# Layer norm, token mixer and MLP on one core: one tile's transpose goes from TensorE to the DMA queue, and every engine gets an explicit order list

## The chip, the cores and the metric

The kernel runs on one core of a Trainium2 chip. The metric is the device time in microseconds (us), the median of three runs. A profile of one execution gives the span from the first to the last instruction, and all rows quoted here are from it.

## What is computed

x is 2048 tokens by 512 features, in bf16; w1 and w2 are 512 by 512, w3 is 512 by 1792, w4 is 1792 by 512.

```
h  = gelu(layernorm(x) @ w1)
g0, g1, g2, g3 = the four quarters of h's features, shifted along the tokens by 1, -1, 2, -2 (zeros come in)
x1 = x + concat(g0, g1, g2, g3) @ w2
out = x1 + gelu(layernorm(x1) @ w3) @ w4
```

## The kernel before

The tokens are cut into 16 tiles of 128. For every tile t there is a first layer norm, numbered t, and a second, numbered 16 + t. A layer norm is a chain of small steps: the statistics (on DVE as bn_stats, L432, and bn_aggr, L434; or for the numbers in STAT_ACT as passes of ACT, L411 and L416, finished on DVE at L421, L424 and L428), the reciprocal root rstd on POOL (L439), then the norm itself: on DVE (L461), or, after a small step nmr (L466), on ACT (L470) or POOL (L473). NORM says which engine, NMR where nmr runs.

A normed tile must be transposed before it can be an operand. Two ways exist. `pe_transpose` turns it on TensorE by four 128x128 transposes (L506) into PSUM, from which EVAC's engine copies it (L514, "both" is half each on ACT and DVE). Or `ln` issues a DMA transpose on SP's queue (L479), named tp and the number. Tiles named in SCRIPT with sa/sb, ty or tp are turned on TensorE: 0 to 7 in this kernel. The other 24 go by DMA.

TensorE's work has five kinds. `mm_up` makes a layer's product with w1 or w3 (L642) for a group of tiles (GROUPS: in the first layer tiles 0 to 4 alone, 5 and 6 together, 7 alone, 8-9, 10-11, 12-15; in the second 0-1, 2-3, 4-7, 8-11, 12-15), in blocks of up to 1024 columns of PSUM, and ACT takes each block through gelu (L657). up1_6 is the first layer's product of group 6, that is of tile 7; up1_7, up1_8 and up1_9 are those of tiles 8-9, 10-11 and 12-15. Tile 0 is done another way round (L544, L610). `mm_mix` multiplies the shifted h of tile t with w2 (L697), and DVE adds x (L709 or L713, named x1_t), after which tile t's second layer norm can run. Because of the shifts, mix t reads the h of its neighbours too. `mm_down` multiplies with w4 (L731), DVE adds x1 (L739), SP sends the result out (L742). Tile 15's down product is cut into pieces of 256, 160 and 96 columns (TAIL). Nine products with zeros stand first on TensorE (warm, L756).

PSUM has three pairs of banks for products and gelu (y_ps) and two banks for mixes, downs and single transposes (o_ps); they are used in turn, so a later step waits for the reader of an earlier one.

SCRIPT sets the order of TensorE's work. LOADS sets the order of the loads on SP (x at L384, weights at L393), with numbers like x4-5 for one load of two tiles. Everything else was ordered by a planner: `order` gives each operation a due time counted back from TensorE's list, BIAS shifts some of them, and `place` then runs through a modelled time (durations, queue and landing models) and picks for each engine the ready operation that is due first. The result is one list per engine; each engine runs its list strictly in order, and waits stand in front of the instruction that needs them (`emit`).

Of the kernel before, what the change touches and what calls it, by code (L numbers as in the profile page):

```python
# [6 lines left out]
P = 128  # L7
# [7 lines left out]
class Op:  # L15


    def __init__(self, name, eng, fn, reads, writes, dur, queue):
        self.name, self.eng, self.fn = name, eng, fn
        self.reads, self.writes = list(reads), list(writes)  # L20
        self.dur, self.queue = dur, queue
        self.idx = 0
        self.descs = 8.0
        self.prio = 1e9
        self.first = None

class Program:

    HOP = {"pe": 200.0, "dve": 155.0, "act": 220.0, "pool": 120.0, "sp": 70.0}
    LOOK = {"dve": 300.0, "act": 300.0}
    DUE = 179877.0
    BEGIN = {"sp": 30.0, "act": 150.0, "pe": 400.0, "dve": 150.0, "pool": 450.0}
    ENTRY = 1900.0
    COLD, RESTART = 4300.0, 800.0
    RING = 150.0
    LAG = {"load": 750, "tp": 350}

    def __init__(self):  # L40
        self.ops = []
        self.lines = []

    def add(self, eng, name, fn, reads=(), writes=(), dur=100.0, queue=None):
        op = Op(name, eng, fn, reads, writes, dur, queue)
        op.idx = len(self.ops)
        self.ops.append(op)
        return op

    def line(self, names):  # L50

        self.lines.append(list(names))

    def order(self):
# [25 lines left out]
        order_only = set()  # L80
        for names in self.lines:
            for a, b in zip(names, names[1:]):
                assert named[a].eng == named[b].eng, (a, b)
                order_only.add((named[a].idx, named[b].idx))
        last = None
        pe_pos = 0
        for op in self.ops:
            if op.eng == "pe":
                if last is not None:
                    preds[op.idx].add(last.idx)  # L90
                last = op
                op.prio = pe_pos
                pe_pos += 1
        order_only = {(a, b) for a, b in order_only if a not in preds[b]}
        for a, b in order_only:
            preds[b].add(a)
        succs = [set() for _ in self.ops]
        for i, d in enumerate(preds):
            for j in d:
                succs[j].add(i)  # L100
        left = [len(s) for s in succs]
        stack = [i for i, n in enumerate(left) if n == 0]
        seen = 0
        while stack:
            i = stack.pop()
            seen += 1
            for j in preds[i]:
                if self.ops[j].eng != "pe":
                    self.ops[j].prio = min(self.ops[j].prio, self.ops[i].prio)
                left[j] -= 1  # L110
                if left[j] == 0:
                    stack.append(j)
        assert seen == len(self.ops), "cycle"
        if self.DUE:

            topo, left = [], [len(d) for d in preds]
            stack = [i for i, n in enumerate(left) if n == 0]
            while stack:
                i = stack.pop()
                topo.append(i)  # L120
                for j in succs[i]:
                    left[j] -= 1
                    if left[j] == 0:
                        stack.append(j)
            due, t = {}, self.DUE
            for op in self.ops:
                if op.eng == "pe" and not op.name.startswith("warm"):
                    due[op.idx] = t
                    t += op.dur
            for i in reversed(topo):  # L130
                op = self.ops[i]
                late = due.get(i, 1e9)
                for j in succs[i]:
                    o = self.ops[j]
                    hop = 70.0 if op.queue else (self.HOP[op.eng] if o.eng != op.eng else 120.0)
                    work = (2300.0 if op.queue == "tp" else op.dur + 1850.0) if op.queue else op.dur
                    late = min(late, o.prio - hop - work)
                op.prio = late
        for op in self.ops:
            op.prio += BIAS.get(op.name, 0.0)  # L140
            if op.first is not None:
                op.prio = op.first
        for names in self.lines:
            for a, b in reversed(list(zip(names, names[1:]))):
                named[a].prio = min(named[a].prio, named[b].prio - 1e-3)

        self.preds = preds
        out = self.place(succs, order_only)
        for a, b in order_only:
            preds[b].discard(a)  # L150
        return out

    def place(self, succs, order_only):

        npend = [len(d) for d in self.preds]
        ready = [0.0] * len(self.ops)
        cands = {e: [] for e in ENGINES}
        for op in self.ops:
            if npend[op.idx] == 0:
                cands[op.eng].append(op)  # L160
        free = dict(self.BEGIN)
        rings = {"sp": [], "act": []}
        fed = {}
        clock = moved = last = turned = self.total = 0.0
        out = []

        def finish(limit):
            nonlocal clock
            while True:
                heads = {e: r[0] for e, r in rings.items() if r}  # L170
                if not heads:
                    return None
                live = [e for e in heads if heads[e][0] <= clock]
                later = min([h[0] for h in heads.values() if h[0] > clock], default=1e18)
                if not live:
                    if later > limit:
                        return None
                    clock = later
                    continue
                first = min(live, key=lambda e: heads[e][1])  # L180
                step = heads[first][1] * len(live)
                ends = clock + step <= min(later, limit)
                if not ends:
                    step = min(later, limit) - clock
                for e in live:
                    heads[e][1] -= step / len(live)
                clock += step
                if ends:
                    return rings[first].pop(0)[2]
                if clock >= limit:  # L190
                    return None

        def release(op, o, at):
            npend[o.idx] -= 1
            if at is not None:
                ready[o.idx] = max(ready[o.idx], at)
            if npend[o.idx] == 0:
                cands[o.eng].append(o)

        def land(op):  # L200
            nonlocal moved, last, turned
            if op.queue == "tp":
                turned = max(clock + 500.0, op.start + 2450.0, last + 500.0, turned + 480.0)
                at = turned + self.LAG["tp"]
            elif op.name.startswith("out"):
                at = clock + 300.0
                self.total = max(self.total, at)
            else:
                moved += op.dur
                at = clock + 600.0 + min(600.0, 0.3 * moved) + (600.0 if op.dur > 1400.0 else 0.0)  # L210
                at += 50.0 if moved <= 1200.0 else self.LAG["load"] - 300.0 if moved <= 4000.0 else self.LAG["load"] if moved <= 11000.0 else self.LAG["load"] + 650.0
            if op.queue != "tp":
                last = max(last, at)
            op.landed = at
            for j in succs[op.idx]:
                if (op.idx, j) not in order_only:
                    release(op, self.ops[j], at + 30.0)

        while len(out) < len(self.ops):
            while True:  # L220
                best = None
                for e in ENGINES:
                    if cands[e]:
                        t = max(free[e], min(ready[o.idx] for o in cands[e]))
                        if best is None or t < best[0]:
                            best = (t, e)
                op = finish(best[0] if best else 1e17)
                if op is None:
                    break
                land(op)  # L230
            t, e = best
            look = self.LOOK.get(e, 1.0)
            op = min((o for o in cands[e] if ready[o.idx] <= t + look), key=lambda o: (o.prio, o.idx))
            cands[e].remove(op)
# [674 lines left out]
```

## Time and profile before

| what | us |
|---|---|
| median of three runs | 135.59 |
| the runs | 135.73, 135.45, 135.59 |
| span of the profiled execution | 133.7 |
| granted TensorE clock, mean | 1.000 |

The profile page gives, per engine, the busy time, its share of the span and the instructions; then the chain of work that ended last, followed back from the end, with shares by engine and by line; then groups of instructions by line. The view of waits lists for one engine the line that waited, the line that released it, the total, the count and the longest. The timeline lists instructions in order of time: start, time to the end of the last of a merged row, engine, line, operation, tiles, count. TensorE's rows overlap, since a product's end is modelled and the next starts before it: there the distance from start to start is what a step takes. Of the DMAs there is a list of issues (out<-in, queue, operation, count, size, median us from issue to landing) and of queues (packets, MB, share of all 16 DMA engines' time in the stretch asked for). Since names of tiles do not tell which tile of 128 tokens a row is, single operations are found by their order on their engine.

| DMAs on SP before, in order | issued at |
|---|---|
| x 0-1, x 2, w1 in two halves | 0.08 to 1.56 |
| x 3, x 4-5, w2 in two halves, x 6, x 7, x 8-10, w3 | 2.16 to 5.54 |
| x 12-13, x 11 | 6.07, 6.68 |
| two transposes, x 14-15 | 14.67, 15.99, 17.29 |
| 16 transposes | 17.91 to 40.79 |
| w4 in two halves | 42.13, 42.75 |
| the other transposes, and outputs | from 43.36 |

### The profile page before, as it was taken

Reading aid. Unit: us, or ns where it says so; the run is one execution under the profiler, and the core shown is the slowest. Engines: PE = TensorE matmul, PEld = TensorE weight load, DVE = VectorE, ACT = ScalarE, POOL = GpSimd, SP = SyncE. Lnnn points to the kernel's source line nnn. Section 1 sums busy time; section 2 is a strip of 40 time slices with the busy share of each in tenths; the row PEclk is TensorE's granted clock in tenths of the full one; section 3 lists DMA queues with packets and bytes.
Section 4 is the critical chain, followed back from the end, with each engine's and each line's share of the span. In section 5 each row is a group of like instructions: output and inputs, shape, how many; then the busy total and the mean of one; then the engine's idle time right before and its main releaser. Section 6 shows DMA issues by size and latency. Waiting matters only on the chain.

```text
span 133.7 us, 2004 instructions
## 1 busy us (share of the span) xinstructions
PE 130.6 (98%) x776; PEld 71.8 (54%) x789; DVE 50.9 (38%) x138; ACT 56.0 (42%) x89; POOL 30.9 (23%) x69
## 2 busy tenths in 40 slices
PE   8999999999999999999999999999999999999994
PEld 3488768874488444444444444444444444444464
DVE  1899998887550830052260003322220000232223
ACT  5699998858657155520025553000006663000000
POOL 2447567696544120012022003100000000000000
PEclk9999999999999999999999999999999999999999
DMA  4999966745442991002211000311111000111112
GB/s 134 329 349 401 237 150 95 83 89 107 98 99 49 295 329 40 0 0 43 77 42 39 0 0 0 78 39 44 39 42 37 0 0 0 39 44 39 39 39 78
DMA packets 21305, 12.19 MB, mean 91 GB/s; under 512 B 13872, under 2 KB 20784, under 8 KB 21296
## 3 DMA queue, kind: packets, MB, share of 16 engines
q1 hardware_dynamic: 20864, 11.93, 32.7%
q10 hardware_dynamic: 432, 0.13, 0.4%
q8 instruction: 6, 0.10, 0.3%
q14 instruction: 3, 0.02, 0.1%
HBM read 6.82 MB, written 2.10 MB: 67 GB/s over the span
## 4 chain that ended last, share of the span: by engine, by line
PE 94%; DMA 2%; DVE 2%; issue 1%; SPq 0%
PE y_ps L642 46%; PE o_ps L731 36%; PE o_ps L697 10%; DMA x_sb<-in_x_dram 2%; PE y_ps L506 1%; DVE st L432 1%; PE y_ps L544 1%; DVE xn_buf L448 0%; DVE xn_buf L461 0%; DVE o_sb L739 0%; PE o_ps L610 0%; DVE mv L434 0%; SPq L894 0%
## 5 line engine op out<-in xcount | busy, mean ns | idle before, releaser
L642 PE MATMUL y_ps<-xnT,w_sb 128*128 128x512 bf16 (+2 forms) x421 | 63.6, 308 | 0.2
L642 PEld LDWEIGHTS y_ps<-xnT,w_sb 128*128 128x128 bf16 x424 | 38.4, 98 | 24.6 <-DVE mv L434 0.2
L731 PE MATMUL o_ps<-w_sb,h2T 128*128 128x512 bf16 (+3 forms) x248 | 48.7, 355 | 0.2
L657 ACT ACTIVATE h2T<-y_ps 128x1024 bf16<-128x1024 f32 (+1 forms) x29 | 28.6, 993 | 47.2 <-PE y_ps L642 47.1
L731 PEld LDWEIGHTS o_ps<-w_sb,h2T 128*128 128x128 bf16 x252 | 23.6, 98 | 25.2
L739 DVE TENSOR_TENSOR o_sb<-o_ps,x_sb 128x512 bf16<-128x512 f32 (+3 forms) x18 | 11.4, 632 | 45.7 <-PE o_ps L731 45.7
L439 POOL TENSOR_TENSOR rstd<-mv,neghalf 128x1 f32<-128x1 f32 x20 | 11.1, 553 | 35.1 <-DVE mv L434 30.1
L697 PE MATMUL o_ps<-w_sb,hT 128*128 128x512 bf16 x58 | 14.8, 379 | 0.3
L432 DVE BATCH_NORM_STATS2 st<-x_sb 128x6 f32<-128x512 bf16 x20 | 13.5, 676 | 2.6 <-DMA x_sb<-in_x_dram 2.5
L713 DVE TENSOR_TENSOR x_sb<-o_ps,x_sb 128x512 bf16<-128x512 f32 x10 | 6.8, 677 | 14.8 <-PE o_ps L697 14.8
L439 POOL TENSOR_TENSOR rstd<-vpe,neghalf 128x1 f32<-128x1 f32 x12 | 6.7, 558 | 15.6 <-DVE vpe L428 15.5
L473 POOL TENSOR_SCALAR xn_buf<-x_sb,rstd,nmr 128x512 bf16<-128x512 bf16 x12 | 9.2, 764 | 1.0 <-DVE nmr L466 0.4
L657 ACT ACTIVATE hT<-y_ps 128x512 bf16<-128x512 f32 (+1 forms) x10 | 8.1, 806 | 3.1 <-PE y_ps L642 2.9
L697 PEld LDWEIGHTS o_ps<-w_sb,hT 128*128 128x128 bf16 x64 | 6.1, 98 | 5.7
L709 DVE SCALAR_TENSOR_TENSOR x_sb<-o_ps,x_sb 128x512 bf16<-128x512 f32 x6 | 4.1, 681 | 12.1 <-PE o_ps L697 12.1
L416 ACT ACTIVATE junk<-x_sb 128x512 bf16<-128x512 bf16 x12 | 7.5, 622 | 2.1 <-DVE x_sb L709 2.0
L461 DVE TENSOR_SCALAR xn_buf<-x_sb,mv,rstd 128x512 bf16<-128x512 bf16 x13 | 6.1, 471 | 2.7 <-POOL rstd L439 2.0
L470 ACT ACTIVATE xn_buf<-x_sb,nmr,rstd 128x512 bf16<-128x512 bf16 x6 | 4.9, 813 | 0.5 <-POOL nmr L466 0.4
L756 PE MATMUL o_ps<-zeros 128*128 128x512 bf16 x9 | 4.0, 631 | 0.4 <-DVE zeros L363 0.4
L411 ACT ACTIVATE junk<-x_sb 128x512 bf16<-128x512 bf16 x6 | 3.7, 624 | 1.2 <-DMA x_sb<-in_x_dram 1.2
L434 DVE BATCH_NORM_AGGREGATE mv<-st 128x2 f32<-128x9 f32 x20 | 3.8, 192 | 0.3
L506 PE MATMUL y_ps<-ident,xn_buf 128*128 128x128 bf16 x32 | 3.4, 236 | 0.2 <-DVE xn_buf L461 0.2
(34 smaller groups left out, 28.7 us busy)
## 6 DMA issues: line engine op xcount, KB each, us to landing
out_dram<-o_sb SPq DMA_DIRECT2D x15, 128.0 KB, 1.7
w_sb<-in_w_dram SPq DMA_DIRECT2D x1, 1792.0 KB, 10.9
w_sb<-in_w_dram SPq DMA_DIRECT2D x2, 896.0 KB, 6.2
x_sb<-in_x_dram SPq DMA_DIRECT2D x4, 256.0 KB, 3.6
w_sb<-in_w_dram SPq DMA_DIRECT2D x4, 256.0 KB, 4.3
x_sb<-in_x_dram SPq DMA_DIRECT2D x5, 128.0 KB, 4.5
x_sb<-in_x_dram SPq DMA_DIRECT2D x1, 384.0 KB, 5.7
xnT<-xn_buf SPq DMA_TRANSPOSE x24, 2.5
```

Of the source, the lines that this page charges most:

```text
L416: (lambda d: (lambda e: e.activation(d, src, ACT_F.Square, accum_out=sums[:, q, 1:2])))(junk[:, b, :]),
L432: pg.add("dve", f"bnst{q}", lambda e: e.bn_stats(st9[:, q, 0:6], src), reads=rs, writes=[(("st", q), 0)], dur=605)
L439: lambda e: e.tensor_tensor(col(rstd), var, neghalf[:], ALU.pow),
L461: lambda e: e.tensor_scalar(dst, src, mv[:, q, 0:1], rstd[:, q : q + 1], ALU.subtract, ALU.mult),
L470: f = lambda e: e.activation(dst, src, ACT_F.Identity, bias=nmr[:, q : q + 1], scale=rstd[:, q : q + 1])
L473: f = lambda e: e.tensor_scalar(dst, src, rstd[:, q : q + 1], nmr[:, q : q + 1], ALU.mult, ALU.add)
L642: ins = e.matmul(y_ps[:, p, W * i : W * (i + 1)], wsb[:, dc, P * fc : P * (fc + 1)], src[:, dc, P * t0 : P * t0 + W], start=(dc == 0), sto ...
L657: (lambda d, s: (lambda e: e.activation(d, s, ACT_F.Gelu_apprx_tanh)))(dst, ysrc),
L697: ins = e.matmul(dst, hT[:, j, c0 : c0 + P], w2_sb[:, j, :], start=(j == order[0]), stop=(j == order[-1]))
L713: f = lambda e: e.tensor_tensor(x1_sb[:, t, :], dst, x_sb[:, t, :], ALU.add)
L731: ins = e.matmul(dst, h2T[:, fc, P * t : P * (t + 1)], w4_sb[:, fc, cs], start=(fc == 0), stop=(fc == FC - 1))
L739: (lambda d, c: (lambda e: e.tensor_tensor(o_sb[:, oi, c], d, x1_sb[:, t, c], ALU.add)))(dst, cs),
```

## The change

Tile 7 is no longer in SCRIPT as a tile for TensorE, so `ln` issues a DMA transpose for it, tp7. It is the first transpose on SP, behind w3 and two loads of x. The last loads of x (tiles 15 and 13) stand behind five transposes. In SCRIPT tile 7's product comes behind mixes 2, 3, 5 and 4 instead of behind mix 3; tile 6 is turned ahead of the fourth product, tile 5 into a bank of o_ps; the blocks of the second layer's products are named one by one (up2:0.4 is group 0, block from 4 on) and stand between mixes and other products. The planner is gone: `order` keeps the dependencies and checks, and takes the order of SP, ACT, DVE and POOL from written lists (ORDER). AHEAD names the operations that are issued ahead of the entry barrier, the same ones as before. The tables NORM, EVAC, STAT_ACT and NMR move statistics and norms between engines. Below is the core; the lists of ACT, DVE and POOL are cut after the first layer's part, and SP's list is whole.

```diff
-        order_only = set()
-        for names in self.lines:
...
-        out = self.place(succs, order_only)
+        lists = {e: [named[n] for n in ORDER[e].split()] for e in ENGINES if e != "pe"}
+        lists["pe"] = [op for op in self.ops if op.eng == "pe"]
...
+            heads = [lists[e][at[e]] for e in ENGINES if at[e] < len(lists[e])]
+            heads = [op for op in heads if preds[op.idx] <= done]
+            op = min(heads, key=lambda op: (op.name not in AHEAD, ENGINES.index(op.eng)))
...
+NORM = {5: "pool", 7: "act", 8: "act", 9: "pool", 10: "act", 12: "pool", 13: "pool", 14: "pool", 19: "pool", 21: "act", 24: "act", 25: "pool", 26: "act", 27: "pool", 28: "act", 30: "pool", 31: "act"}
+EVAC = {0: "dve", 1: "act", 2: "dve", 3: "both", 4: "both", 5: "dve", 6: "both"}
+STAT_ACT = (0, 5, 7, 9, 10, 12, 16, 18, 20, 22, 24, 25, 26, 27, 28)
+NMR = {5: "pool", 7: "pool", 8: "pool", 9: "pool", 12: "pool", 14: "pool", 19: "pool", 21: "pool", 25: "pool", 26: "pool", 27: "pool", 30: "pool", 31: "pool"}
...
-x0-1 x2 tp2 w1a w1b x3 x4-5 w2b w2a tp5 x6 tp6 x7 x8-10 tp4 w3 x12-13 tp0 x11 tp17 x14-15 tp26 tp5 w4a tp3
-w4b
+x0-1 x2 w1a w1b w2b w2a w3 w4a w4b x4-5 x14 x13 x7 x15 x3 x6 x8-10 x11-12
...
-warm:9 sa:0 sb:0 ty:1 ra:0 rb:0 ty:2 up1:1 th:0 up1:2 mix:0 ty:3 mix:1 ty:4 up1:3 ty:5 up1:4 ty:6 mix:2
-up1:5 ty:7 mix:3 up1:6 mix:5 mix:4 up2:0 up1:7 mix:6 up1:8 mix:7-8 up1:9 mix:10 mix:9 up2:1 mix:13 mix:11
-up2:2 mix:14 down:2 down:1 down:0 mix:12 up2:3 mix:15 down:3 down:5 down:7 down:4 down:6 down:10 up2:4
-down:8 down:11 down:9 down:12-15
+warm:9 sa:0 sb:0 ty:1 ra:0 rb:0 ty:2 up1:1.0 th:0 up1:2.0 ty:3 mix:0 mix:1 ty:4 ty:6 up1:3.0 tp:5 up1:4.0
+up1:5.0 mix:2 mix:3 mix:5 mix:4 up1:6.0 up2:0.0 mix:6 up1:7.0 up2:0.4 up2:0.8 mix:8 up1:8.0 mix:7 up2:0.12
+mix:9 mix:10 up1:9.0 up1:9.2 up2:1.0 up2:1.4 mix:15 mix:13 up2:1.8 mix:12 up2:2.0 mix:11 up2:2.2 mix:14
+up2:1.12 down:0 down:1 down:2 up2:2.4 up2:2.6 up2:2.8 up2:2.10 up2:3.0 up2:2.12 up2:3.2 up2:4.0 up2:3.4 down:7
+down:3 up2:3.6 up2:3.8 up2:4.2 up2:3.10 down:4 up2:4.4 down:5 up2:3.12 up2:4.6 up2:4.8 down:8 up2:4.10 down:11
+down:6 down:10 up2:4.12 down:9 down:12 down:13 down:14 down:15
...
+    "sp": """
+dma_x0 dma_x2 dma_w1a dma_w1b dma_x3 dma_x4 dma_x6 dma_w2b dma_w2a dma_x7 dma_x8 dma_w3 dma_x11 dma_x14 tp7
+tp16 tp17 tp9 tp8 dma_x15 dma_x13 tp11 tp10 tp12 tp15 tp14 tp13 tp18 tp19 tp22 tp23 tp21 tp20 dma_w4b tp26
+dma_w4a tp25 out_dma1_0 tp30 tp28 tp24 tp27 tp31 tp29 out_dma0_0 out_dma3_0 out_dma5_0 out_dma4_0 out_dma7_0
+out_dma2_0 out_dma6_0 out_dma10_0 out_dma8_0 out_dma11_0 out_dma9_0 out_dma13_0 out_dma14_0 out_dma12_0
...
+    "act": """
+warm_gelu sum0 ssq0 ev1 gelur0 ssq5 gelu1_1_0 sum5 gelu1_2_0 ev3act ssq7 sum7 sum9 ev4act ssq16 ev6act
+gelu1_3_0 norm7 ssq9 gelu1_4_0 gelu1_5_0 sum10 ssq18 sum12 norm8 ssq12 gelu1_6_0 ssq20 ssq10 gelu2_0_0 norm10
+ssq22 norm21 gelu1_7_0 gelu2_0_8 gelu2_0_4 ssq24 gelu1_8_0 gelu2_0_12 norm24 ssq26 ssq25 gelu1_9_0 gelu1_9_2
...
+    "dve": """
+zeros bnst1 bnag1 bnst2 norm0_0 norm0_1 norm1 bnag2 ev0_0 msq0 ev0_1 vpe0 norm2 bnst3 bnag3 ev2 bnst4 norm3
+evh0 bnag4 bnst6 msq5 bnag6 vpe5 ev3dve norm4 norm6 x1_0 msq7 ev4dve vpe7 mean16 bnst8 ev6dve ev5 x1_1 msq16
+vpe16 bnst17 bnag17 msq9 norm16 bnag8 vpe9 norm17 x1_2 x1_3 bnst19 bnag19 mean18 x1_5 x1_4 mean20 msq18 bnst21
+msq10 bnag21 bnst11 msq20 vpe20 bnag11 vpe18 msq12 vpe10 bnst14 norm20 x1_6 nmr10 norm11 vpe12 bnst15 mean22
+msq22 bnag15 norm18 vpe22 bnag14 bnst13 norm15 bnag13 x1_8 nmr13 mean24 msq24 norm22 vpe24 nmr24 x1_7 bnst23
...
+    "pool": """
+trip0 trip1 neghalf ident0 epsc pad0 ident1 pad1 rstd1 rstd2 rstd0 rstd3 rstd4 rstd6 rstd5 nmr5 norm5 rstd7
+nmr7 rstd16 rstd17 rstd9 rstd8 nmr9 nmr8 norm9 rstd19 nmr19 norm19 rstd21 rstd20 rstd10 rstd11 rstd18 nmr21
+rstd12 nmr12 norm12 rstd14 rstd15 nmr14 norm14 rstd13 rstd22 norm13 rstd24 rstd23 rstd25 nmr25 norm25 rstd26
...
```

In these lists bnst and bnag are bn_stats and bn_aggr, sum, ssq, mean, msq and vpe the steps of the statistics on ACT and DVE, ev a copy out of PSUM, and dma_x11 the load that begins with tile 11.

## The prediction

> **What bounds it.** I read the busy shares and the chain that ended last first, then what PE waited for, then PE's timeline.
>
> ```profile
> PE 130.6 (98%) x776; PEld 71.8 (54%) x789; DVE 50.9 (38%) x138; ACT 56.0 (42%) x89; POOL 30.9 (23%) x69
> ...
> PE 94%; DMA 2%; DVE 2%; issue 1%; SPq 0%
> ```
>
> ```profile
> PE o_ps L756 <- DVE zeros L363: 0.4, 1, 0.4
> PE y_ps L506 <- DVE xn_buf L461: 0.2, 1, 0.2
> ```
>
> The first fence says that PE is busy for 98% of the span and is 94% of the chain. The second is PE's whole list of waits: 0.4 us before its first instruction and 0.2 us before tile 1 is turned. From 5.12 us to its last product PE waits for nothing. So only work taken from PE, or a shorter head or tail, can make this kernel faster; everything else can only add waits. The timeline of PE gives the price of each step (first column the start, second the time to the modelled end, so the start of the next line is what counts).
>
> ```profile
> 9.64 1.03 PE L697 MATMUL o_ps<-w_sb,hT 128*128 128x512 bf16 x4
> 10.50 0.39 PE L506 MATMUL y_ps<-ident,xn_buf 128*128 128x128 bf16 x4
> 10.72 1.06 PE L642 MATMUL y_ps<-xnT,w_sb 128*128 128x128 bf16 x16
> 11.62 0.39 PE L506 MATMUL y_ps<-ident,xn_buf 128*128 128x128 bf16 x4
> ...
> 13.82 1.91 PE L642 MATMUL y_ps<-xnT,w_sb 128*128 128x256 bf16 x16
> 15.57 0.39 PE L506 MATMUL y_ps<-ident,xn_buf 128*128 128x128 bf16 x4
> ```
>
> From start to start: a mix 0.86, turning a tile 0.22, a first-layer product of one tile 0.89, sixteen products 256 wide 1.75 (eight: 0.87).
>
> **What is removed: 0.22 us.** Tile 7 is no longer turned on PE: four transposes, 0.22 us (10.50 to 10.72), all of it on the path. Its copy out of PSUM (ACT or DVE, under 0.7 us) was beside PE and is worth nothing. The Trainium skill ("TensorE: Matmul & The Clock Gate", Part 4: PE-mode transpose) gives about 275 ns for one 128x128 transpose inside a kernel; by that the change would save 1.1 us. The row shows four in 0.22 us, because each starts 0.056 us after the one before, and the row decides.
>
> The head keeps its end. On DVE bn_stats of tile 2 now runs ahead of the two halves of tile 0's norm, but the same instructions stand before tile 1's norm, so PE's wait still ends at 5.12. Tile 0's copies move from ACT to DVE and end near 5.37 and 5.75; their products started at 5.45 and 5.89, so this costs nothing between bounds of 0 and 0.1. The last four down products and the three pieces of the tail are as before, so the tail is worth 0. The planner is gone from the program text only; no instruction on the chip goes with it.
>
> **What is moved: deadlines.** Up to the second group's product (end 8.55) PE does the same as now. I add the prices above in the new order, without waits: tile 5 is turned at 11.84, up1_5 starts 12.96, mix 2 at 14.70, up1_6 (tile 7) at 18.15, up2_0 (its first block) at 19.05, up1_7 (tiles 8, 9) at 21.66, up1_8 (tiles 10, 11) at 27.75, up1_9 (tiles 12 to 15) at 32.96. Each of these starts now waits for something with little room, and I work out each from rows.
>
> Tile 5's norm moves to POOL, behind the rstd of tiles 6 and 5:
>
> ```profile
> 9.39 0.55 POOL L439 TENSOR_TENSOR rstd<-vpe,neghalf 128x1 f32<-128x1 f32 x1
> 10.04 0.26 POOL L466 TENSOR_SCALAR nmr<-mv,rstd 128x1 f32<-128x1 f32 x1
> ...
> 11.00 0.26 POOL L466 TENSOR_SCALAR nmr<-mv,rstd 128x1 f32<-128x1 f32 x1
> 11.37 0.76 POOL L473 TENSOR_SCALAR xn_buf<-x_sb,rstd,nmr 128x512 bf16<-128x512 bf16 x1
> ```
>
> An rstd is followed by its nmr after 0.65, that by the norm after 0.37, and the norm takes 0.76. Tile 6's bn_aggr ends on DVE near 9.56, so the two rstd start at 9.62 and 10.14, nmr 10.79, norm 11.16 to 11.92, plus 0.07 to PE: **0.15 late**.
>
> Transposes on SP come next. An issue takes 1.31 from one to the next; in an empty queue it lands 2.5 after its issue. Behind copies it is held:
>
> ```profile
> 14.67 1.27 SPq L479 DMA_TRANSPOSE xnT<-xn_buf  x1
> ...
> 22.36 1.27 SPq L479 DMA_TRANSPOSE xnT<-xn_buf  x1
> ...
> 26.01 1.26 SPq L479 DMA_TRANSPOSE xnT<-xn_buf  x1
> ```
>
> ```profile
> x_sb<-in_x_dram SPq DMA_DIRECT2D x1, 128.0 KB, 10.8
> ...
> xnT<-xn_buf SPq DMA_TRANSPOSE x1, 3.4
> ...
> q8 instruction: 1, 0.02, 7.1%
> xnT<-xn_buf SPq DMA_TRANSPOSE x1, 4.2
> ...
> xnT<-xn_buf SPq DMA_TRANSPOSE x1, 2.5
> ```
>
> The second of these fences shows issue to landing (last number). The last x load was issued at 6.7 and landed at 17.5; the transpose of 14.67 landed at 18.07, 0.6 behind it. The one of 26.01 took the plain 2.5, the one of 22.36 took 4.2, in a stretch with an instruction fetch on one DMA engine (7.1% of 16 engines over 1.3 us: that engine's whole time).
>
> In the new list the same bytes stand ahead of the transposes (the three first weights and 14 tiles of x), so the copies again end at 17.5. Tile 7's norm is on ACT, behind 0.48 (gelu), 0.30 (half copy) and 0.61 (statistics pass) steps from 8.87 on; I add them to a norm from 13.17 to 13.98. Then tp7 is issued at 14.03, tp16 15.34, tp17 16.65, tp9 17.96, tp8 19.27. They land at 18.1, 18.5, 19.15, 20.5, 21.8. With 0.06 to PE: tp7 on time for 18.15, tp17 0.15 late for 19.05, tp8 **0.16 late** for 21.66. x15 and x13 are issued behind tp8 and no longer hold it; that is the cover which this order buys. The bound for tp7: if it issued at once it is still held to 18.1; if ACT is 0.5 later it still is; beyond that all five shift alike.
>
> tp11 waits for tile 11's norm on DVE. From the start of tile 3's add (16.79, after mix 3) to the end of that norm stand four adds of 0.65, four bn_stats (2.48 with one wait), three bn_aggr 0.31, a norm 0.32, nine small ones 1.06, nmr 0.13 and the norm's 0.41: 7.31, so 24.1. The small ones are 0.07 each back to back and 0.25 where one reads the one before; these bounds make 0.63 to 2.25 of the nine, and the end 23.7 to 25.3. I take 24.1, nearest to back to back, as most of them read older results. tp11 then issues at 24.13, tp10 25.44, landing 27.93: **0.24 late** for 27.75 (bounds: 0.2 early to 1.4 late). tp12, tp15, tp14, tp13 follow at 1.31 each, the last at 30.68, landing 33.17: **0.27 late** for 32.96. Queued behind are tp18 to tp20, with 0.9 us or more of room.
>
> These are not added: a wait of PE at one place moves PE to where the next only asks for the rest, since the SP queue and DVE run on by their own chains. The largest counts: 0.27 us of waits in all.
>
> Further on I find room. w4's halves are issued near 40.0 and 41.9 and took 5.2 and 7.2 from issue to landing, so 49.1 against the first down at 50.8. The first output, which waits for down 1, stands ahead of six transposes, issued from 58.3 on; tp27, the fourth, lands 64.7 against 66.7. Blocks of up2 on PE take 1.73 and their gelu 1.02, as now. The outputs reuse four buffers in an order that leaves 0.5 us or more. One DMA more (one transpose, and one load more from the new cut of x) is in queues already counted.
>
> **Sum.** -0.22 + 0.27 = +0.05 on the profiled span of 133.73 us. The profile gives no other time for this execution; I take the 1.86 between this span and the median of the runs, 135.59, as unchanged, which makes **135.64**. Anything within 0.27 us (0.2%) is no change for a measurement of this kernel: the three runs spread over 0.28.
>
> **Rivals.** First, the waits are covered: if DVE's small ones run at 0.07 and POOL at the pitch of two rstd, 0.52, only the 0.22 remains, 135.37, still within 0.2%. For it: four of five lateness figures are under 0.25, about my rows' rounding along a chain. Against it: five places would all have to turn out early. It is also the floor, as PE has nothing else to lose, so a clear gain needs the measurement's own spread.
>
> Second, on the other side: an instruction fetch on one DMA engine holds a transpose that PE now waits for. The row of 22.36 prices it: 4.2 - 2.5 = 1.7; the one of 19.15 (3.9, partly behind a load) 1.4 at most. In the stretch from 20 to 22 us there are two fetches of 8 KB now, half the size. tp8 and tp9 move their packets there in the new order, and PE has no room, where today up1_7 starts at 25.5, some 2.5 us after its tiles landed. I take 0.9, between nothing and 1.7: 0.16 + 0.9 - 0.22 = +0.85, 136.4; with the full 1.7 on tp10, 0.24 + 1.7 - 0.22, 137.3. It decides from 0.5 us of lateness on. Against it: a fetch follows the count of instructions, which the new order shifts by some tenths of a us. The Trainium skill ("Runtime: NRT & Kernel Launch", Instruction fetch mechanics) calls crossing a 16 KiB block of instructions mostly hidden, which would price this rival at nothing; the transpose of 22.36 shows otherwise for whoever shares the DMA engine.
>
> Third, the change might not do what it says: tp7 late enough to cost the 0.22 it saves. It is held to 18.1 in any case and up1_6 comes at 18.15 to 18.3, so this needs 0.3 us more on the loads, as when w3 is later: 135.7, inside the forecast's own range.
>
> **Chances.** Forecast 0.45 (135.45 to 135.9), no waits 0.20, a held transpose 0.30, others 0.05. Faster by over 0.2% takes 0.08 from the second and 0.02 from others: 0.10. Slower takes 0.30, 0.05 from the forecast's top and 0.03 from others: 0.38. Same: 0.52. The range leaves out the upper half of the held case and the spread below the floor: 135.3 to 136.8.
>
> **What would show it.** PE with four transposes fewer at L506; a wait of about 0.15 there on POOL near 11.9; waits at L642 on DMAs near 18 to 19, 21.7, 27.8 and 33, summing to 0.3 or less. One wait of 0.7 or more at 21.7 or 27.8, with a transpose that took over 3 us to land, is the second rival. Waits of PE after 40 us, on w4 or on h2T, would be something I have missed.

## The result, and the profile after

The changed kernel takes **136.72 us** (four runs, 136.66 to 136.82) against 135.52 (135.34 to 135.73): a ratio of 1.0092 with an interval of 1.0076 to 1.0108, so it is slower by 1.2 us. That is inside the predicted range (135.3 to 136.8), but at its upper end, on the side of the second rival and not of the forecast, which was no change.

The page of the changed kernel, engine by engine and then the chain by engine:

```profile
PE 131.2 (97%) x772; PEld 71.1 (53%) x785; DVE 48.2 (36%) x145; ACT 58.2 (43%) x96; POOL 28.5 (21%) x66
...
PE 86%; DMA 7%; DVE 2%; SPq 1%; issue 1%
```

What TensorE waited for (line, releaser, total us, times, longest us):

```profile
PE y_ps L477 <- DMA xnT<-xn_buf: 0.8, 2, 0.4
PE o_ps L590 <- DVE zeros L203: 0.4, 1, 0.4
PE y_ps L344 <- DVE xn_buf L287: 0.4, 1, 0.4
```

The chain gives PE 86% where it gave 94%, and DMA 7% where it gave 2%. The new line in the list of waits is the first: two waits of products (L477) for DMA transposes. The timeline of PE says which (start, time to the modelled end, idle time before in brackets):

```profile
18.96 1.06 PE L477 MATMUL y_ps<-xnT,w_sb 128*128 128x128 bf16 x16
20.42 1.91 PE L477 MATMUL y_ps<-xnT,w_sb 128*128 128x256 bf16 x16 [0.40 <-DMA xnT<-xn_buf]
22.17 1.03 PE L531 MATMUL o_ps<-w_sb,hT 128*128 128x512 bf16 x3
23.55 0.72 PE L477 MATMUL y_ps<-xnT,w_sb 128*128 128x256 bf16 x5 [0.35 <-DMA xnT<-xn_buf]
```

These are up1_6 (tile 7, on time), up2_0 and up1_7. The brackets are shorter than what is lost, because a product's modelled end runs past the next one's start: by start-to-start distance up2_0 comes 0.57 late (20.42 instead of 18.96 + 0.89) and up1_7 0.52 (23.55 instead of 22.17 + 0.86). From 24 us to the last product PE does not wait any more.

The whole account of the two profiled executions, by PE's steps: the last product starts 1.67 later. The removed transposes are worth -0.22. Mix 0 waits 0.26 for its half of w2 (landed at 9.75, 8.43 before), tile 5's turn and mix 5 about 0.15 together, up2_0 0.57, up1_7 0.52, and tile 0's products start 0.25 later (5.70 against 5.45). That is 1.53; the rest is small gaps. Not all of it is owed to the change, since the executions of one kernel differ and before's profiled one was a fast one. In every run since, the time is about 1.33 above the span, so its span of 133.73 stands for some 135.1 and not for the median. Its loads came early: w1's first half landed at 4.74, but at 5.08 to 5.67 in 12 of the 13 other profiles told of here, whatever the head of the kernel. And mix 0 waits over 0.1 for w2 in none of the others. The waits for transposes are most of what is left.

SP's queue shows where the two waits begin. Five transposes, tp7, tp16, tp17, tp9, tp8, merged in one row, and the first two of them alone:

```profile
14.46 7.15 SPq L317 DMA_TRANSPOSE xnT<-xn_buf  x5
```

```profile
14.46 3.23 SPq L317 DMA_TRANSPOSE xnT<-xn_buf  x2
```

At the 1.31 per issue of the profile before, five would take 6.5 and two 2.6. The second issue, tp16's, is held: 1.92 instead of 1.27. All that follows is 0.65 later, so tp17 lands at 20.29 while PE stands ready at 19.86; 0.65 earlier it would have been in time. The DMA queues from 14.4 to 18 us (queue, packets, MB, share of 16 engines; then issues, with the median us to landing):

```profile
q14 instruction: 1, 0.01, 1.8%
q8 instruction: 1, 0.02, 1.8%
...
xnT<-xn_buf SPq DMA_TRANSPOSE x3, 3.8
```

Two fetches of instructions, each 1.8% of 16 engines over 3.6 us, so about 1 us of one engine; the 16 KB one starts at 15.59, right ahead of the held issue. Then tp8, issued at 20.35, takes 3.1 to land instead of 2.5. The queues from 21.5 to 23.6 us:

```profile
q14 instruction: 1, 0.01, 0.9%
...
xnT<-xn_buf SPq DMA_TRANSPOSE x1, 3.1
```

The fetch of 8 KB starts at 21.93, in the middle of tp8's packets. Of the 544 packets of transposes that start between 21.5 and 22.85, the median takes 0.02 us; 13 take over 0.3 us, and all of these end at 22.8. Beside the 16 KB fetch it is alike: 14 of tp7's packets take 0.9 to 1.2 us and all end at 17.5, and tp16's issue ends at 17.69.

Is it chance that a held issue has a fetch beside it? In the 14 profiles of the kernels told of here 235 transposes are issued between 12 and 40 us. 27 of the issues took over 1.45 us, and **in each of the 27 a fetch was under way**, in 24 of them one of 16 KB:

| issues of transposes | held (over 1.45 us) | not held |
|---|---|---|
| a fetch of 16 KB under way | 24 | 10 |
| a fetch of 8 KB alone | 3 | 29 |
| no fetch | 0 | 169 |

Of the ten with 16 KB that were not held, seven met the fetch only in their last 0.3 us, two only in their first 0.5, and one took 1.45. The kernel before has one too, 2.27 us at 23.69 beside the fetch of 23.43; no product was due there. Its earlier 16 KB fetch, from 14.10 to 15.16, fell on the first 0.5 us of its first issue and held nothing.

### The profile page after: what moved, and what is told of

Same layout as the page of the kernel before. It is cut to its first block, busy times and chain, and to the rows that moved or that the text cites. A ratio compares the mean times of both kernels' runs of the same rounds, so it can differ in the third digit from the quotient of the medians.

```text
span 135.4 us, 2006 instructions
## 1 busy us (share of the span) xinstructions
PE 131.2 (97%) x772; PEld 71.1 (53%) x785; DVE 48.2 (36%) x145; ACT 58.2 (43%) x96; POOL 28.5 (21%) x66
## 3 DMA queue, kind: packets, MB, share of 16 engines
HBM read 6.82 MB, written 2.10 MB: 66 GB/s over the span
## 4 chain that ended last, share of the span: by engine, by line
PE 86%; DMA 7%; DVE 2%; SPq 1%; issue 1%
PE y_ps L477 42%; PE o_ps L565 36%; PE o_ps L531 8%; DMA w_sb<-in_w_dram 4%; DMA xnT<-xn_buf 2%; DVE x_sb L547 1%; SPq L224 1%; DVE st L271 1%; DVE x_sb L543 0%; PE y_ps L344 0%; SPq L233 0%; PE o_ps L344 0%; DVE o_sb L573 0%; DVE mv L273 0%; DVE mv L260 0%
## 5 line engine op out<-in xcount | busy, mean ns | idle before, releaser
L477 PE MATMUL y_ps<-xnT,w_sb 128*128 128x512 bf16 (+2 forms) x420 | 64.7, 308 | 1.0 <-DMA xnT<-xn_buf 0.8
L477 PEld LDWEIGHTS y_ps<-xnT,w_sb 128*128 128x128 bf16 x424 | 38.0, 98 | 26.3 <-DMA xnT<-xn_buf 1.2
L565 PEld LDWEIGHTS o_ps<-w_sb,h2T 128*128 128x128 bf16 x252 | 23.6, 98 | 25.0
L271 DVE BATCH_NORM_STATS2 st<-x_sb 128x6 f32<-128x512 bf16 x17 | 11.5, 677 | 2.9 <-DMA x_sb<-in_x_dram 2.6
L278 POOL TENSOR_TENSOR rstd<-mv,neghalf 128x1 f32<-128x1 f32 x17 | 9.3, 548 | 14.8 <-DVE mv L273 13.4
L278 POOL TENSOR_TENSOR rstd<-vpe,neghalf 128x1 f32<-128x1 f32 x15 | 8.5, 571 | 9.2 <-DVE vpe L267 5.9
L255 ACT ACTIVATE junk<-x_sb 128x512 bf16<-128x512 bf16 x15 | 9.3, 622 | 2.6 <-DVE x_sb L543 2.5
L308 ACT ACTIVATE xn_buf<-x_sb,nmr,rstd 128x512 bf16<-128x512 bf16 x8 | 6.5, 806 | 4.2 <-POOL nmr L304 3.3
L311 POOL TENSOR_SCALAR xn_buf<-x_sb,rstd,nmr 128x512 bf16<-128x512 bf16 x9 | 7.0, 776 | 1.7 <-DVE mv L260 1.0
L543 DVE SCALAR_TENSOR_TENSOR x_sb<-o_ps,x_sb 128x512 bf16<-128x512 f32 x9 | 6.2, 687 | 2.4 <-PE o_ps L531 2.3
L547 DVE TENSOR_TENSOR x_sb<-o_ps,x_sb 128x512 bf16<-128x512 f32 x7 | 4.8, 686 | 5.0 <-PE o_ps L531 5.0
L250 ACT ACTIVATE junk<-x_sb 128x512 bf16<-128x512 bf16 x6 | 3.7, 619 | 1.3 <-DMA x_sb<-in_x_dram 1.3
L304 POOL TENSOR_SCALAR nmr<-mv,rstd 128x1 f32<-128x1 f32 x13 | 3.4, 264 | 0.8
```

Source lines behind the costliest of these rows:

```text
L255: (lambda d: (lambda e: e.activation(d, src, ACT_F.Square, accum_out=sums[:, q, 1:2])))(junk[:, b, :]),
L271: pg.add("dve", f"bnst{q}", lambda e: e.bn_stats(st9[:, q, 0:6], src), reads=rs, writes=[(("st", q), 0)])
L278: lambda e: e.tensor_tensor(col(rstd), var, neghalf[:], ALU.pow),
L308: f = lambda e: e.activation(dst, src, ACT_F.Identity, bias=nmr[:, q : q + 1], scale=rstd[:, q : q + 1])
L311: f = lambda e: e.tensor_scalar(dst, src, rstd[:, q : q + 1], nmr[:, q : q + 1], ALU.mult, ALU.add)
L477: ins = e.matmul(y_ps[:, p, W * i : W * (i + 1)], wsb[:, dc, P * fc : P * (fc + 1)], src[:, dc, P * t0 : P * t0 + W], start=(dc == 0), sto ...
```

## The experiments

| kernel | us | ratio to before | interval |
|---|---|---|---|
| changed | 136.72 | 1.0092 | 1.0076 to 1.0108 |
| changed, tile 7 on TensorE | 135.83 | 1.0037 | 1.0016 to 1.0057 |
| the same, tile 5 and tile 0 undone too | 136.10 | 1.0034 | 1.0010 to 1.0059 |
| before, tile 7 by DMA | 135.95 | 1.0041 | 1.0018 to 1.0064 |
| before, tile 7 by DMA and the gap filled | 136.78 | 1.0113 | 1.0089 to 1.0137 |
| changed, w2 ahead of x6 | 137.28 | 1.0128 | 1.0107 to 1.0149 |
| changed, 64 tiny instructions more | 136.13 | 1.0053 | 1.0033 to 1.0073 |
| changed, x14 later | 136.67 | 1.0096 | 1.0075 to 1.0116 |
| both of these | 136.50 | 1.0088 | 1.0068 to 1.0108 |
| changed, tile 0's head as before | 136.48 | 1.0084 | 1.0062 to 1.0106 |
| changed, tile 5's norm on DVE | 136.59 | 1.0082 | 1.0061 to 1.0103 |
| changed, products later | 137.96 | 1.0189 | 1.0163 to 1.0215 |
| the same, mended | 137.17 | 1.0136 | 1.0100 to 1.0172 |

The runs came in several rounds on several chips, and the kernel before ran in each round; its medians went from 135.29 to 135.52. Kernels of different rounds are therefore compared by their ratio to it.

The theory at the outset: the loss is the time for which PE waits for late transposes. Rivals: the loss is in the other moved work; the largest wait alone counts.

**Undo the move alone.** In the changed kernel tile 7 is turned on PE again:

```diff
-up1:5.0 mix:2 mix:3
+up1:5.0 mix:2 ty:7 mix:3
```

> The changed kernel with tile 7 turned on TensorE again, between mix 2 and mix 3, and copied by DVE; tp7 is gone from SP's list, the rest of the new lists stays. Theory A (tp7 at the head pushes every later transpose back by one issue of 1.31 us, so the first block of up2_0 and up1_7 wait 0.57 and 0.52 us in the profile of the changed kernel): both waits go, the four transposes cost 0.22 again, so 136.72 - 1.09 + 0.22 = 135.85. Theory B (the moved lists cost by themselves: head, w2 behind x6, tile 5's norm on POOL): the waits stay, 136.9.

135.83: by the medians 0.89 of the 1.2 us is the move itself, by the ratios 0.75. It takes away 0.22 of PE's work, so by this difference some 1 us of waits came with it. The other 0.3 to 0.45 is not explained by it. The number is theory A's, but in the profile only the wait at up2_0 is gone. That execution, the slowest of its twelve (137.19), shows that the rest of the order is tight as well, with transposes late at up1_7 and up1_8:

```profile
23.46 5.41 PE L477 MATMUL y_ps<-xnT,w_sb 128*128 128x256 bf16 x48 [0.29 <-DMA xnT<-xn_buf]
28.93 0.81 PE L531 MATMUL o_ps<-w_sb,hT 128*128 128x512 bf16 x3
30.11 1.16 PE L477 MATMUL y_ps<-xnT,w_sb 128*128 128x256 bf16 x9 [0.37 <-DMA xnT<-xn_buf]
```

**The move alone in the old kernel.** Here the planner is kept, tile 7 goes by DMA, and its product comes behind mix 4.

```diff
-x7 x8-10 tp4 w3 x12-13 tp0 x11 tp17
+x7 x8-10 tp4 w3 x12-13 tp0 x11 tp7 tp17
-up1:5 ty:7 mix:3 up1:6 mix:5 mix:4
+up1:5 mix:3 mix:5 mix:4 up1:6
```

> The kernel before with tile 7 alone changed: tp7 as the first transpose on SP, its product behind mix 4, everything else by the old planner. Theory A: the third transpose (tp17) lands between 19.5 and 20.3 where TensorE wants it at 19.05, up1_7 has 2 us of room; 135.52 - 0.22 + 0.5 to 1.2 = 135.8 to 136.5, with one wait at the first block of up2_0 and none elsewhere. Theory B: the order of SP's queue is not the cause, only the 0.22 is seen, 135.3.

135.95, 0.41% slower, with less moved than in the change. That is in theory A's range, but mostly by luck, since what is late is something else: mix 5 now follows mix 3 directly, and waits for the gelu of tiles 5 and 6.

```profile
17.67 1.89 PE L697 MATMUL o_ps<-w_sb,hT 128*128 128x512 bf16 x8 [0.41 <-ACT hT L657]
```

The tile's turn and its product (1.1 us of PE) had been the cover of that gelu. By start-to-start 0.58 is lost there and 0.22 at up2_0, where tp17 lands late.

**Instruction fetches moved.** 24 tiny instructions more on DVE, 24 on POOL and 16 on ACT, early in their lists; nothing is left out.

```diff
+for eng, n in (("dve", 24), ("pool", 24), ("act", 16)):
...
-zeros bnst1 bnag1
+zeros fill_dve0 fill_dve1
...
```

> The changed kernel with tiny instructions that write to a scratch tile (24 on DVE and 24 on POOL while they wait for the first load, 16 on ACT, 8 of them there and 8 behind tile 0's statistics); they do nothing but move each engine's place in its instruction stream, so that instruction fetches fall some us earlier. Theory F (an instruction fetch on one DMA engine holds tp8, which landed 3.15 us after its issue where 2.5 is usual): the fetch of 21.93 is gone from there, tp8 takes 2.5, the wait of 0.52 at up1_7 shrinks to 0.1 or less, about 136.3. Theory G (the transposes wait for the queue, not for fetches): nothing moves, 136.7.

136.13: **more instructions made the kernel faster by 0.5 to 0.6 us** (by ratios and by medians; the intervals do not meet). The fetches now start at 14.56 to 15.14 and at 21.08, and tp8 (issued 20.49) lands in the plain time. The fetch of 21.08 now meets tp9, which takes 3.1 from its issue at 19.18 and still lands at 22.31, ahead of tp8. Queues from 21.0 to 23.0, and PE:

```profile
xnT<-xn_buf SPq DMA_TRANSPOSE x1, 2.5
```

```profile
20.55 1.91 PE L491 MATMUL y_ps<-xnT,w_sb 128*128 128x256 bf16 x16 [0.56 <-DMA xnT<-xn_buf]
22.29 1.03 PE L545 MATMUL o_ps<-w_sb,hT 128*128 128x512 bf16 x3
23.16 1.04 PE L491 MATMUL y_ps<-xnT,w_sb 128*128 128x256 bf16 x8
```

The wait at up1_7 (23.16, 0.87 after mix 6) is gone. The wait at up2_0 stays and is even longer, 0.72, so that the last product of this profiled execution starts 0.41 earlier than in the changed kernel's; the medians gain somewhat more. It is longer because the 16 KB fetch, 0.9 earlier now (14.70), meets tp7's issue instead of tp16's and holds it by 1.0:

```profile
14.24 2.28 SPq L331 DMA_TRANSPOSE xnT<-xn_buf  x1
```

**Is the issue held by the load of x14?** It is put behind tp17, alone and together with the 64 instructions.

```diff
-dma_x11 dma_x14 tp7 tp16 tp17 tp9 tp8
+dma_x11 tp7 tp16 tp17 dma_x14 tp9 tp8
```

> The changed kernel with the load of x 14 moved from ahead of tp7 to behind tp17. In the profile of the changed kernel SP's issue of tp16 took 1.92 us where 1.27 is usual, and tp17 landed at 20.29, 0.52 after TensorE wanted it. Theory Q (too many descriptors stand in the queue ahead, so SP is held while it issues): tp16 issues in 1.3, tp17 lands 0.6 earlier, the wait at the first block of up2_0 falls from 0.57 to near 0, and 136.72 becomes 136.2. Theory F2 (the one DMA engine with the instruction fetch at 15.6 sets the landing of tp7 and tp16, whatever stands in the queue): the hold and the wait stay, 136.6 to 136.7.

> Both edits at once: the filler instructions of e4_fillers (136.13, the wait at up1_7 gone, 0.72 left at up2_0) and x 14 behind tp17. If queue and fetch are two causes with a wait each, the wait at up2_0 goes too: 135.6. If x 14 is not what holds SP, 136.1.

136.67: no, theory F2's number. tp7's issue (14.05) is held instead, 2.05, with the fetch at 14.55; three waits for transposes remain.

```profile
PE y_ps L477 <- DMA xnT<-xn_buf: 1.1, 3, 0.5
```

With both, 136.50, a miss of either expectation. In the profile, of the fastest of its six executions (136.17), tp7's issue is held by 0.3 only and the wait at up2_0 is down to 0.07, yet up1_7 waits 0.50: the issue of x14 takes 0.6 us of SP ahead of tp9 and tp8.

**The early waits.** w2 goes ahead of x6; tile 0's two half norms go ahead of tile 2's statistics, with their copies on ACT; tile 5's norm goes to DVE.

```diff
-dma_x4 dma_x6 dma_w2b dma_w2a
+dma_x4 dma_w2b dma_w2a dma_x6
```

> The changed kernel with the load of x 6 behind the two halves of w2, as before. In the profile of the changed kernel mix 0 waits 0.26 us for the second half of w2. Theory A1 (tile 7's norm, and with it the transposes, hang on TensorE's progress): all that follows comes 0.26 earlier, 136.45. Theory A2 (the transposes are held by the queue of DMAs whatever TensorE does): the wait at mix 0 goes and comes back at the first block of up2_0, 136.7.

```diff
-EVAC = {0: "dve", 1: "act"
+EVAC = {1: "act"
-zeros bnst1 bnag1 bnst2 norm0_0 norm0_1
+zeros bnst1 bnag1 norm0_0 norm0_1 bnst2
```

> The changed kernel with the head of the kernel before: the halves of tile 0's norm ahead of bn_stats of tile 2 on DVE, tile 0's copies out of PSUM on ACT. My prediction priced this part at 0 to 0.1: 136.6 to 136.7. If the first products now start later because of it (5.70 against 5.45 in the two profiles), up to 0.25 comes back: 136.45.

```diff
-norm4 norm6 x1_0
+norm4 norm6 norm5 x1_0
```

> The changed kernel with the normalization of tile 5 on VectorE, right behind that of tile 6, and no longer on GpSimd. Theory W (each wait adds): the turn of tile 5, 0.1 to 0.23 late now, is on time, and all behind it comes as much earlier: 136.45 to 136.6. Rival S (what is won there is swallowed by the transposes that come next, since their landing does not hang on TensorE): 136.7, with the wait at up2_0 longer by what was won. VectorE's later work moves by 0.33 at most; if that delays a copy or an add, over 136.8.

The first came out at 137.28, slower than both theories said: mix 0 does not wait, as in the other profiles, but tile 6's turn does (0.31), and up2_0, up1_7 and up1_8 wait 0.36, 0.49 and 0.76. The other two, 136.48 and 136.59, lie 0.24 and 0.13 below the changed kernel by the medians and 0.11 and 0.14 by the ratios, within their intervals. In the last one's profile tile 5 is turned on time, but the wait at up2_0 grew to 0.67, as rival S had it, and the copy behind the norm on DVE is now late for the same tile's product:

```profile
13.54 0.72 PE L477 MATMUL y_ps<-xnT,w_sb 128*128 128x256 bf16 x5 [0.18 <-DVE xnT L352]
```

**Products later, transposes as they are.** One block of up2_0 goes ahead of up1_7 and one ahead of up1_8.

```diff
-mix:6 up1:7.0 up2:0.4 up2:0.8 mix:8 up1:8.0 mix:7 up2:0.12
+mix:6 up2:0.4 up1:7.0 up2:0.8 up2:0.12 up1:8.0 mix:8 mix:7
```

> The changed kernel with one block of the first wide product (up2_0 from 4) put ahead of up1_7, and another (from 12) ahead of up1_8 with mixes 8 and 7 behind it, so that tiles 8/9 are due 1.75 us later and tiles 10/11 about 1.7 us later; up2_0's own start is left where it is. No transpose is moved. Theory W (the loss is the time that TensorE waits for late transposes, and waits at different places add): the waits at up1_7 and up1_8 (0.4 to 0.5 each where they show) go, the one at up2_0 (0.55) stays: 135.9 to 136.3. Rival L (the largest wait alone counts, so that the first wait at up2_0 already costs nearly all, and the later ones merely move): 136.5 to 136.8. Rival G (the new order brings waits of its own, for a gelu or a bank): over 136.9, with waits that are not for DMAs.

137.96: the waits for tiles 8 to 11 are gone, and rival G took their place, because lists written for the old order run an add and a gelu late.

```profile
PE o_ps L531 <- DVE x_sb L547: 1.6, 1, 1.6
PE y_ps L477 <- ACT h2T L492: 0.7, 1, 0.7
...
PE y_ps L477 <- DMA xnT<-xn_buf: 0.3, 1, 0.3
```

The two waits come to 2.6 us in a profiled execution of 138.89, the slowest of its six; that leaves some 136.3. The next expectation takes them from the median, 137.96, and so starts too low. Then ACT's and DVE's lists were mended:

> The changed kernel with the order of products of the run before last (one block of up2_0 ahead of up1_7, another ahead of up1_8, mixes 8 and 7 behind up1_8) and without the two waits that were of that order's own making: the gelu of the moved block stands right behind the normalization of tile 10 on ScalarE, and the adds of mixes 8 and 7 follow each other on VectorE, with the normalization of tile 13 ahead of them. That order stood at 137.96, and 2.6 us of its profile were those two waits (0.8 for a gelu, 1.8 for a bank), so that 135.3 to 135.5 would be left without them. Theory W (each wait for a transpose costs what it shows; taking two of the three away is worth their 0.9 to 1.0): 135.6 to 136.0, with the wait at up2_0 (0.5 to 0.6) as the only one over 0.3 for a DMA. Four mixes in a row may cost 0.1 to 0.3 for their banks, which is in that range. Rival L (the largest wait alone counts, or the loss is elsewhere): 136.5 to 136.8, though the two waits are gone.

137.17, a miss. No wait for a transpose is over 0.3, but the two statistics passes ahead of up1_9's gelu on ACT, which stood there before, now wait for an add until 37.81 (36.34 in the changed kernel), and a product waits for its pair of banks:

```profile
40.11 1.92 PE L477 MATMUL y_ps<-xnT,w_sb 128*128 128x256 bf16 x16 [0.63 <-ACT hT L492]
```

0.8 by start-to-start. Without it some 136.4 would be left of the median, between the two theories, and 136.0 of the profiled execution (136.79), the top of theory W's range; this run does not decide.

**Can the move pay in the old kernel?** Tile 7 by DMA, mix 2 behind up1_5, tile 6 turned earlier, x6 ahead of w2, and x11 behind the first three transposes.

```diff
-w3 x12-13 tp0 x11 tp17 x14-15
+w3 x12-13 tp0 tp7 tp17 x11 x14-15
-up1:3 ty:5 up1:4 ty:6 mix:2 up1:5 ty:7 mix:3 up1:6 mix:5
+up1:3 ty:5 ty:6 up1:4 up1:5 mix:2 mix:3 mix:5 mix:4 up1:6
```

> The kernel before with tile 7 by DMA, and with what e2_tp7_in_before lacked: there mix 5 waited 0.58 for the gelu of tiles 5 and 6, since neither tile 7's turn nor its product stood between. Here mix 2 stands there instead, tile 6 is turned ahead of the fourth product with its norm on DVE and its load ahead of w2, and x 11 and x 14-15 go behind tp17. If the move is worth its 0.22 once its waits are covered: 135.3, below both kernels. If SP still brings tp17 too late for up2_0 (three issues of 1.31 and 2.5 to land, from tile 7's norm near 14.4, make 19.5 against 19.1): 135.7.

136.78, a miss. Mix 5 and up2_0 wait under 0.1 now. Instead up1_4 waits 0.4 for a gelu (at 12.81), and up1_8 waits for a transpose that is issued only at 27.06, 1.0 by start-to-start:

```profile
29.69 1.47 PE L642 MATMUL y_ps<-xnT,w_sb 128*128 128x256 bf16 x12 [0.84 <-DMA xnT<-xn_buf]
```

An issue shortly ahead of it, at 23.68, was held beside a fetch (2.02 us), which makes 0.75 of this. In five of the profiles told of here up1_8 waits over 0.4 for a transpose, and in each of them its issue, or one of the two ahead of it, had been held. That the late x11 put this transpose so far back is likely, but not shown.

**Three parts undone together**, with the explicit lists kept:

> The changed kernel with three of its parts undone and its explicit lists kept: tile 7 turned by TensorE between mixes 2 and 3 again, tile 5 normalized on VectorE, tile 0's halves normalized ahead of tile 2's statistics and copied by ScalarE. Alone they gave 135.83 (tile 7), 136.59 (tile 5) and 136.48 (tile 0) against 136.72. Theory P (the parts add, and nothing else in the change costs): 136.72 less 0.89, 0.13 and 0.24, 135.46, within 0.15% of the kernel before. Rival Q (the lists themselves, with the x loads and the transposes as they stand, cost some 0.3, which shows as waits at up1_7 or up1_8 that none of the three removes): 135.7 to 135.9.

136.10 in twelve runs, not 135.46, and 135.83 with tile 7 alone was no worse. By the ratios, 1.0034 against 1.0037, undoing tile 5 and tile 0 as well gave nothing; but the sum of the three parts by ratios, 1.0019, lies inside the interval, so theory P is not reached and not excluded. In its profile the 16 KB fetch (14.60 to 15.64) is over before the first transpose is issued (15.91), no issue is held until 30, and no product waits over 0.2 for a transpose. What it has is 0.31 for the same late copy on DVE as with tile 5's norm there. Both kernels without tp7 stand above the kernel before, with intervals clear of 1: some 0.3 to 0.6 us of the change do not hang on tile 7, and which part of the lists they come from is open.

## Where the prediction was right and where it was wrong, point by point

**Bound, removed work, later stages: right.** PE was the bound; four transposes are 0.22 (each 0.056 from start to start, in both profiles). w4, the later transposes and the outputs never came late.

**The head at 0 to 0.1: right, as far as the runs show.** Tile 0's products start 0.25 later, but w1's first half landed at 5.42 instead of 4.74. The last of tile 0's four products starts at 6.44 to 6.69 in the four later profiles with the old head and at 6.19 to 6.82 in the nine with the new one, and undoing the head gave 0.11 to 0.24, within its interval.

**The moved norm of tile 5: about right.** 0.15 was forecast, 0.05 to 0.23 measured in the profiles.

**SP's transposes: the step that failed.** The forecast had five issues 1.31 apart from 14.03 and tp17 landing 0.15 after PE's need. The issues ran 14.46, 15.78, 17.74, 19.04, 20.35. The start was 0.43 later, since ACT reached tile 7's norm later, and the second issue was held by 0.65. The profile before had such an issue, 2.27 us at 23.69, and the prediction read only the rows of 1.27. It also read the 7.1% as an engine's whole time in its window of 1.3 us; that fetch began at 23.43, near the window's end, and ran to 24.90, beside the held issue. tp17 landed 1.14 later than forecast and PE came 0.8 later, which makes 0.15 + 1.14 - 0.8 = 0.49 of the 0.57. For tp10 and tp13 0.24 and 0.27 were forecast; PE was some 1.9 late by then (up1_8 at 29.66) and waits for neither.

**"These are not added: the largest counts": wrong, for a reason that the runs show.** The argument was that a wait for tp17 gives tp8 time. With the fetch moved off tp8 it does, and one wait is left. In the changed kernel tp8 was itself held, so a second wait of 0.52 came on top. The sum of waits was 0.27 by the forecast; up2_0 and up1_7 alone make 1.09.

**The second rival: this is what came, in two places and not one.** It had a fetch hold one transpose in flight, priced 0.9, 136.4. One fetch held tp8 in flight by 0.6; the other, of 16 KB, stood beside tp16's issue and put 0.65 on all behind it. The prediction looked at the two fetches of 8 KB between 20 and 22 us and did not ask where the 16 KB one of 14.1 would fall once the order changed. The 64 instructions show that tp8's part is worth 0.5 to 0.6 us. That the sum, 136.4, came near 136.72 is partly luck: it had one long hold where two short ones came, and not the part of the loss that stays without tp7. The Trainium skill ("Runtime: NRT & Kernel Launch", Instruction fetch mechanics) calls the crossing of a 16 KiB boundary of the instructions mostly hidden; for the DMA transposes of this kernel it was not, as the 27 held issues and tp8 show.

**tp7 too late (third rival): no, but by luck.** tp7 landed at 18.91, 0.8 later than forecast and 1.3 behind the last copy instead of 0.6; up1_6 started at 18.96, since PE was 0.8 late as well.

**The base.** The 1.86 us taken to lie outside the span are 1.33; the profiled execution was faster than the median. The forecast was made from the median, so this did not move it; but the rows that it was summed from are those of an execution of some 135.1, with early loads.

What stays open: by what means a fetch holds an issue (that the hold follows the fetch from tp16 to tp7, and that a few packets stand still beside it, is shown, no more), and the 0.3 to 0.6 us of the lists. A version that beats the kernel before was not found.

## What to carry to other kernels

Taking work from a saturated engine is worth no more than its start-to-start price, here 0.22 us; giving it to a queue whose items come due one after the other with hardly any room cost more than that here. Count as room only what is left after one held issue (0.2 to 1.0 us here) and one held transfer (0.6 us), at every due time in the queue, and look up where the instruction fetches fall. When an order is tight, a changed list shifts the wait to the next place: undo one part alone and look which line of the waits takes its place.

## What was not expected of the hardware

The issue of a DMA transpose, 1.27 us by itself, took 1.5 to 2.3 us in 27 of the 66 cases in which a fetch of instructions was under way, and in none of the 169 others; the queue behind a held issue slides (0.65 us in the changed kernel). 64 tiny instructions more, off the critical path, made a kernel 0.5 to 0.6 us faster; in its profile the fetches moved, and the transposes that they held with them. And executions of one kernel differ by up to 1.6 us in 136 (135.57 to 137.19, the last one profiled), so one profile shows which waits are possible, and only the medians what they cost.
